# A written-out order of 1700 operations is replaced by another one, with 23 warm-up matmuls in it where there were 20

## The chip, the cores and the metric

The kernel runs on one core of one Trainium2 chip. The metric is the device time of one execution in microseconds (us), the median of three runs for the kernel before.

## The reference, cut to what matters

One transformer-like layer on a sequence of 2048 positions with 448 features, in bf16. A conditioning row `c` gives six modulation vectors; then come a windowed attention with 16 heads and a gMLP mixer, each on a modulated layernorm and added back through a gate.

```python
mod = (silu(c) @ w_mod)                 # 448 -> 6 x 448: sa, ca, ga, sb, cb, gb
h = layernorm(x) * (1 + ca) + sa
q, k, v = split(h @ wqkv)               # 16 heads of 28
p = softmax(q k^T / sqrt(28))           # only keys 0..255 positions back
x = x + ga * ((p v) @ wo)
h = layernorm(x) * (1 + cb) + sb
z = gelu(h @ w_in)                      # 448 -> 1792
z1, z2 = z[:, :896], layernorm(z[:, 896:])
g = w_sp @ z2 + b_sp[:, None]           # 2048 x 2048 over the positions
x = x + gb * ((z1 * g) @ w_out)
```

## The kernel before, in words

Everything stays on the chip between the first loads and the stores. The sequence is cut into 16 tiles of 128 positions, and these into six blocks of 1, 1, 2, 4, 4 and 4 tiles (blocks 0 to 5).

The kernel first records about 1720 operations, each with its engine, its inputs and the buffers that it takes, and then gives them out in the order of one long table, `ORDER` (lines 179 to 239). An entry `35` is operation number 35; `73.1` is operation 73 in its second form, which is mostly another engine; `71/3` also says which buffer it takes. Every engine runs its operations strictly in the order in which they stand in the table, and an operation waits by semaphore for its inputs and for the last users of its buffers. So the table decides three things: what stands behind what on each engine, which engine does a movable operation, and which buffer it uses. The DMAs stand in the queue of SyncE (SP), and two of the first ones in that of ScalarE.

The names below are those that the kernel gives its operations.

- **Start.** GpSimd (POOL) sets constants: `warm` (L539, the operand of the warm-up matmuls), `id1` (`ident`, L542), `zo0` and `zo1` (`zero_one`, L541), `one` (L540). TensorE (PE) runs `warm0` and so on, which multiply zeros and whose result nobody reads; they are recorded at lines 1257 to 1260 and depend only on the memset of `warm` and on each other. `c_cols` turns `c` into columns. `wmodA01` and `wmodA23` (L508 on SP, L510 on the queue of ACT) load the first two modulation vectors, `wqk03` and `wqkM` (L514, L515) weights, `x0`, `x0b` and `x1` (L500) the first tiles.
- **modA**, 16 operations of two matmuls of one column each, makes the first modulation vectors from the loaded weights; VectorE (DVE) turns them into `modT` (L596).
- **tr0, tr1**: normalized tiles `xn` are transposed by matmul with `ident`; ACT or DVE apply the modulation and write `hT` (L695, L700).
- **qk0, qk1, ...**: queries and keys of a block, in pieces over the feature chunks; the first read `wqk_raw` (L781), the others `WQK`, a spread-out copy that ACT, DVE and POOL make (L735 to L737). `qke` moves a result from PSUM to `QKT`. `v` and `ve` are the same for the values.
- **S, E, M, PV**: scores on PE, the exponential on ACT (L902), the mask on POOL (L905), the product with the values on PE (`arena,Vaug`). Then `oq`, `rec`, `nrm`, `oT` on DVE (L1073 to L1082; `nrm` may go to POOL), `wo` on PE and `x1_` on DVE (L1092).
- **Mixer**: second layernorm and transposes by DMA, `z2m` and `z1m` on PE, gelu on ACT (L1149, L1168), layernorm over 896 features (`l3_`, `z2n`); `woutg` (L883) multiplies the rows of `w_out_sb` by the gate `gB_sb` on POOL or DVE.
- **G**: `G<tb>_<ft>_<quarter>`, 112 operations of four matmuls of 512 columns, the product with `w_sp`, whose 32 pieces `wsp<tb>_<p>` are loaded and transposed by DMA (L1197) into `QKT`, `w_spC` and `w_spD`. Then `ga` and `gu` on DVE (L1226, L1228), the matmuls `out`, `fin` on DVE (L1248) and the stores.

PE takes its work in **four shapes**. Most matmuls use the whole array. A column-split operation is issued as four matmuls of 32 columns of weights, one beside the other (L466, L781, and all PV). A score matmul uses four strips of 28 rows. The last 64 of the 448 features give matmuls of 64 rows, `..._r`, two of which can share the array where one uses the upper and the next the lower half; they may also be done over the whole array with zeros. After the table has been read, `column_tiles` makes each whole-array operation of a free kind column-split when it stands in one stretch with PV operations:

```python
if o is not None and o.mode in (FREE, COLS):
    seg.append(o)
    continue
if any(x.mode == COLS for x in seg):
    self.cols.update(x.seq for x in seg)
```

Of the kernel before, what the change touches and what calls it, by code (L numbers as in the profile page):

```python
# [179 lines left out]
21 25 22 24 27 28 1 2 0 3 4 8 6 7 23 36 35 34 15 32 67 68 69 26 70 71/3 31 1701/0 1702 1703 1704 1705 1706 1707 1708 37/4 1709 1710 33 38 39 40/1 41  # L180
42 43 44 45 46 47 48 49 50 51 52 53 54 55 78/7 72/6 56 73.1 79 1711 1712 1713 74/1 75 58.1 62.2 63.2 125 126 127 76/0 77.1 11 182 128 129 130.1/2 60.1
65.1 61.1 5 64.1 90/3 85/4 1714 80/2 1715 95/7 96 115/1 81 86 87 116 97 117 105/0 106 98 88 91 82 92 83 93 180 99.1 183 181 84.1 184 185 66.1 89 107
108 118 57 133/7 131/6 1716 1717 94 109 119 134 500/0,0 502/1 1718 1719 1720 132.1 135/2 160/0 150/1 151 136 59 137 138 139 152 165/3 161 162 153 154
166 167 163 164 168 169 110/1 100/3 111 112 113 101 114 102 103 104 145/2 146 147 148 149 155/1 156 157 158 159 140/3 141 142 143 144 501/1,1 505/0
170/2 171 172 186 187.1/3 192/3 188.1/4 193 194 190/1 173 12 10 9 14 13 189 120/6 121 122 247 249 251 245 252 246 250 248 253 174.1 517/1,0 518/6
521/7 503 30.1 175/2 176 177 123 178 179 191.1 225/1 227 228 226 494/3 124 18 19 20 17 16 254 255 256/1 260 334 229.1 524/1,0 525/8 527/5 328 495.1
413 215/1 195/2 198 197 196 205/0 199.1 207 206 208 209.1 259.1/4 263 257.1/3 258.1/2 262 506 29 519 522 498 499 261 200/3 217 202 203 216 201 204
220/2 222 221 230/0 332 411 335 330 218.1 223.1 224 333 219.1 329 331 538/0,1 540/5 539/1 232 210/3 231 211 240/2 242 233.1 243.1 213.1 241 234.1 212
235/1 238 237 336 337 264 541/0,1 504/0 236 507 267 266 265 338 214 244 542 543 544 508/0 341/4 239.1 509 339.1/1 343 340/0 510/1 342/2 415 323/3
278/2 279 324 281 280 282 325 326 327 546/0,1 547/4 550/2 548/1 545 549 551/0 552 288/2 289 268/3 270 291 290 303/1 292 305 520/0 269 523 528 526  # L190
529/0 553/1,0 555/4 554/0 271.1 306.1 272.1 283/2 304 307 273/0 275 274 308/3 286.1 311.1 276.1 511/1 530 531.1/1 416 417 277.1 497.1 414 556/0,1 557
558 559 309 298/1 301 310 312.1 564/0 299 300 302 561 284 565 293/3 285 287 532/2 496.1 560 418 412 419 420 562 591/0,1 593/3 592/2 563 512/1 566
573/0 574 533/2 534 535 536 513 294 514 515 296 571/0 295 575.1/0 537 594/1,0 516 576/1 912 346 344 345 350.2 297.1 568 570 572 567 569 582/0 595 597
577/1 578 579 580 581 599/2,1 603/0 600/4 421 583 347.1 349.1 376/0 348.1 378 361/1 377 379.1 364.1 606/1,0 607/5 424/1 584/0 380.1 363 362 365.1
585/2 913 909 428 911 910 381/0 382 384 383 385.1 608/4 366/1 609/1,2 610 369 368 367 370.1 596 598 604/2 601/1 605 602 615/0 617 618 614 612 644/1,0
646/1 645/0 586/1 587 588 589 948 944 590 318/3 320 356/2 357 319 611 616 613 619 396/1 321.1 322 359.1 399.1 946 626/0 627 647/1,0 650 648 358 360.1
397 926/0 398 927 928 929 930 931 932 652/2,0 653/3 949 400.1 945 947 423.1/3 422.1/4 628.1/0 425.1/2 629/2 649 651 933 934 313/1 314 316 620/0 315
656/1 623 659/1,2 661/2 621 624 950 317.1 625 622 951 635/0 636 952 637/1 654/2 657/4 655 658 660/4 351/1 352 353 354 355 406/2 371/3 386/0 389.1
409.1 662/0,1 665 666 663 664 407 408 388 373 387 638/0 390.1 372 639/1 640 641 642 410.1 643 916 1433 919 1435 427 426 429 431.2 697/0,1 699/5 374
670/0 671 668 375.1 433.1 430.1 667 401/1 669 672 679/0 680 953 404.1 432 681.1/0 698/3 700/2,1 701 403 402 405.1 630/0 631 632 633 634 705/0,2 954  # L200
967 454/1 455 456 457 458.1 673/0 676 675 678 677 674 688/0 682/0 703 702 704 709/0 710/1 706/2 707/4 711 712/1,2 713/0 391/1 394 392 393 689 395.1
955.1/2 690/1 961.1/0 449/0 451 450 714/1 715/0,1 716 717 718 719 683/1 684 444/3 685 686 687 691/2 920 1434 922 956 921 464/2 466 465 467.1 452.1 453
447.1 750/0,1 752/2 446 445 726/0 434/1 727 730 731 729 708 728 968 468.1 448.1 741/0 742 957/1 751/4 753/1,2 756 435 436 437 438.1 692/0 693 694 695
696 959/2 743.1/1 744/1 973 971 969 970 757 754 755 758/0,2 759/3 722/0 723 725 762/1 459/1 462.1 724 765/1,0 460 461 463.1 972 767/0 766/5 469/2 470
721 720 732/0 974 760/0 761 763/2 764 479/3 481 480 482.1 472.1 483 768/1,0 769 733 975 734.1/1 770 439/1 471 473.1 484/0 485 486 442.1 487.1 488.1
771 772 803/2,1 804/1 735/0 917 914 962 960 958 964.1 441 440 443.1 773/0 777 774 776 775 778 785/0 786 805/3 806/0,2 809 745/1 746 747 976 965 787/0
736/0 737 738 739 740 966.1 807 808 811/2,1 815/4 788/0 748 749 977 782/0 781 779 783 784 780 794/0 816/0 984.1/1 915 918 985 812/3 813/1 810 963.1
789/1 818/1,0 820/4 819/0 790 791 792 795 793 796.1/0 474/0 476 475 477 478.1 821/0,2 822 935/1 936.1 980.1/2 830/0 827 826 829 824 856/1,0 857/5
858/2 1077/1 1078 1079 1043/2 1045 1044 1080 1046 797/1 798/3 799 1051.1 800 801 992 994 1085 995 802 996 859/0,1 860 823 814 828 489/2 1047/1 491 825
978/1 817 1060/3 861 862 863 982.2/0 925 1442 981 979 923 983 924 1444 1443 1048 1062 1049 831 490 1061 1050 1063 1068.1 838/0 839 840.1/0 1052  # L210
864/0,1 868/2 837/0 834 835 832 836 833 1098/3 1099 1064/1 1100 1066 1065 1101 492.1 990 847/0 997 993 841/1 848 869/1 865/3 866/4 867 1103.1 1067
1069 493.1 991 871/0,1 873/0 872/4 986.1 989.2 1081/0 1083 842/3 843 844 845 846 1094/1 1096 1082 1308/7 1095 998 999 1097 1084 1102.1 987 988 1086
1000 849/1 1007.1/1 1013 850/2 941.1 1001/2 1002 1008 874/2,0 1310 875 876 877 1104/1 1313/6 1315 1314 1303/3 1305 1304 1309 1338/1 1339 1340 879/0
1162/0 1158 1164 882 1311 1161 1306 1341 1342 1316 1317 1307 1165 851/2 852 853 854 855 1014 1015 1105 878 870 1003/0 883 1160 881 1159 1115/3 1116
1117 880 884 1111/2 1328/3 1329 1343/6 1113 1112 1330 1345 1163 1016 891/0 1106 892 1005/2 940 1053/0 1312 1166/2 938 893/1 1017 1055 894/0 1018 888/0
1331 1114 1346 1119.1 1118 886 1348/7 1344 1132/0 1134 885 890 887 1350 1128 1347 1120.1 1332 1004 1006 1019 1020.2/2 1009.2 1012.2 1446 1022/1 1023
# [1101 lines left out]
```

## Time and profile before

| | us |
|---|---|
| median of 3 runs | 265.5 |
| lowest and highest | 264.46, 266.9 |
| the profiled execution's own time | 266.06 |
| its span, first to last instruction | 264.3 |
| mean granted TensorE clock | 0.987 |
| PE busy | 258.9 |
| DVE busy | 162.7 |
| ACT busy | 128.9 |
| POOL busy | 102.2 |

The profile shows one execution. Its own time is 1.76 us above its span, since the time also holds what lies before the first and after the last instruction. A busy PE is not a PE at its peak: a matmul counts as busy from its start to its modelled end, and they overlap, so what a matmul costs is read from the distance between the starts of one and the next.

### The profile page before, as it was taken

How to read it: one execution, taken by the hardware profiler on the slowest of the kernel's cores; microseconds unless marked ns; L12 is line 12 of the kernel's file. 1: busy time of each engine (PE TensorE's matmuls, PEld its weight loads, DVE VectorE, ACT ScalarE, POOL GpSimd, SP SyncE). 2: the span in 40 equal slices, each digit the busy share in tenths (PEclk: the TensorE clock that was granted, in tenths of full speed). 3: DMA queues.
4: the chain of work that ended last, by engine and by line, in shares of the span. 5: the costliest groups of instructions: out<-in, count | busy, mean ns of one | idle time of the engine just before them, and what ended most of it. 6: DMA issues, size and time to landing. Idle time of an engine off the chain costs nothing.

```text
span 264.3 us, 7779 instructions
## 1 busy us (share of the span) xinstructions
PE 258.9 (98%) x3401; PEld 129.5 (49%) x3401; DVE 162.7 (62%) x392; ACT 128.9 (49%) x183; POOL 102.2 (39%) x151
## 2 busy tenths in 40 slices
PE   6999999999999999999999999999999999999996
PEld 2676554656445454544444444444444444444453
DVE  4688999879888887879796713714105344152273
ACT  4699998999999999876886100000000000000000
POOL 3469679779788968784431400000000000000000
PEclk9599999999999999999999999999999999999999
DMA  6953251972390755557999990000000000000014
GB/s 220 360 172 82 58 130 28 200 132 65 69 167 28 135 82 133 101 99 142 182 167 209 181 182 0 0 0 2 0 0 0 2 0 17 17 2 17 0 59 166
DMA packets 61022, 23.86 MB, mean 90 GB/s; under 512 B 49854, under 2 KB 60861, under 8 KB 60989
## 3 DMA queue, kind: packets, MB, share of 16 engines
q1 hardware_dynamic: 60715, 22.92, 42.0%
q8 instruction: 26, 0.43, 0.7%
q10 hardware_dynamic: 274, 0.46, 0.5%
q14 instruction: 7, 0.06, 0.1%
HBM read 9.47 MB, written 1.84 MB: 43 GB/s over the span
## 4 chain that ended last, share of the span: by engine, by line
PE 95%; DMA 2%; ACT 1%; DVE 0%; issue 0%; SPq 0%; DVEq 0%
PE ps L469 82%; PE ps L466 12%; DMA wmod_sb<-in_w_mod_dram 2%; ACT arena L902 1%; PE ps L781 1%; DVE hT L700 0%; SPq L500 0%; DVE fin L1248 0%; DVE modT L596 0%; DVEq L172 0%
## 5 line engine op out<-in xcount | busy, mean ns | idle before, releaser
L902 ACT ACTIVATE arena<-ps 128x1024 bf16<-128x1024 f32 x76 | 72.3, 1031 | 2.3 <-PE ps L469 2.1
L1226 DVE TENSOR_TENSOR tmpg<-ps,bsp_bc 128x512 bf16<-128x512 f32 x28 | 19.2, 690 | 58.4 <-PE ps L469 58.4
L469 PE MATMUL ps<-QKT,z 128*128 128x512 bf16 x224 | 51.9, 379 | 0.0
L905 POOL TENSOR_SCALAR_AFFINE_SELECT arena<-arena 128x512 f32<-128x512 f32 x60 | 40.3, 687 | 13.3 <-ACT arena L902 11.4
L469 PEld LDWEIGHTS ps<-QKT,z 128*128 128x128 bf16 x224 | 21.9, 98 | 26.2
L619 POOL TENSOR_TENSOR rs_all<-ve_all,neghalf 128x1 f32<-128x1 f32 (+2 forms) x27 | 19.3, 716 | 26.5 <-DVE ve_all L618 26.3
L469 PE MATMUL ps<-w_spD,z 128*128 128x512 bf16 x112 | 27.1, 379 | 0.0
L469 PE MATMUL ps<-w_spC,z 128*128 128x512 bf16 x112 | 26.9, 379 | 0.0
L469 PE MATMUL ps<-w_in_sb,hT 128*128 128x448 bf16 (+1 forms) x100 | 25.1, 353 | 0.0
L469 PE MATMUL ps<-hT,w_in_sb 128*128 128x512 bf16 (+1 forms) x88 | 23.6, 379 | 0.0
L469 PE MATMUL ps<-w_out_sb,z1T 128*128 128x448 bf16 (+2 forms) x119 | 23.0, 342 | 0.0
L611 DVE BATCH_NORM_STATS2 st_all<-z2raw 128x6 f32<-128x448 bf16 x32 | 18.8, 613 | 4.5 <-ACT z2raw L1149 3.2
L469 PE MATMUL ps<-hT,WQK 128*128 128x128 bf16 (+4 forms) x127 | 21.4, 299 | 0.0
L611 DVE BATCH_NORM_STATS2 st_all<-x_sb 128x6 f32<-128x448 bf16 x32 | 18.9, 614 | 0.2
L822 DVE CAST QKT<-ps 128x512 bf16<-128x512 f32 (+2 forms) x25 | 14.5, 584 | 6.1 <-PE ps L469 3.5
L1168 ACT ACTIVATE z1T<-ps 128x512 bf16<-128x512 f32 x28 | 15.6, 598 | 4.9 <-PE ps L469 4.9
L469 PE MATMUL ps<-arena,Vaug 128*32 128x128 bf16 x720 | 17.9, 221 | 0.1
L469 PE MATMUL ps<-QKT 28*64 28x64 bf16 (+3 forms) x944 | 17.7, 211 | 0.1
L469 PEld LDWEIGHTS ps<-w_spC,z 128*128 128x128 bf16 x112 | 11.0, 98 | 13.2
L1248 DVE TENSOR_TENSOR fin<-ps,x_sb 128x448 bf16<-128x448 f32 (+2 forms) x17 | 9.8, 594 | 12.2 <-PE ps L469 12.1
L469 PEld LDWEIGHTS ps<-w_spD,z 128*128 128x128 bf16 x112 | 11.0, 98 | 12.8
L469 PEld LDWEIGHTS ps<-arena,Vaug 128*32 128x32 bf16 x720 | 13.5, 95 | 6.6 <-issue 0.8
(98 smaller groups left out, 344.4 us busy)
## 6 DMA issues: line engine op xcount, KB each, us to landing
wmod_sb<-in_w_mod_dram SPq DMA_DIRECT2D x8, 224.0 KB, 4.5
w_in_sb<-in_B_w_in_dram SPq DMA_DIRECT2D x8, 224.0 KB, 3.8
out_dram<-fin SPq DMA_DIRECT2D x16, 112.0 KB, 1.7
x_sb<-in_A_x_dram SPq DMA_DIRECT2D x3, 448.0 KB, 7.8
bsp_bc<-in_B_b_sp_dram SPq DMA_DIRECT2D x1, 512.0 KB, 4.1
wqk_raw<-in_A_wqkv_dram SPq DMA_DIRECT2D x1, 452.0 KB, 6.1
wmod_sb<-in_w_mod_dram SPq DMA_DIRECT2D x1, 448.0 KB, 5.1
wmod_sb<-in_w_mod_dram ACTq DMA_DIRECT2D x1, 448.0 KB, 5.2
```

The costliest lines, as they stand in the source:

```text
L466: last = e.matmul(out_[32 * j:32 * j + 32], lhsT=lhsT[:, 32 * j:32 * j + 32], rhs=rhs, start=st, stop=sp, tile_position=(0, 32 * j), **kw)
L469: return e.matmul(out_, lhsT=lhsT, rhs=rhs, start=st, stop=sp, **kw)
L611: st = [dve("%sst%d" % (name, i), prio, dve_ns(D), lambda e, i=i, s_=s_: e.bn_stats(st_all[:, slot, t, i, :], s_()), deps, tens) for i, s_ ...
L619: r = pool(name + "rs", prio, 420 + 148 * n, lambda e: e.tensor_tensor(rs_all[:, slot, t0:t1], ve_all[:, slot, t0:t1], neghalf[:, t0:t1], ...
L781: last = e.matmul(out_[32 * j:32 * j + 32], lhsT=lhsT[j], rhs=rhs, start=st, stop=sp, tile_position=(0, 32 * j))
L822: return e.tensor_copy(QKT[:, g, cols], ps[:, ten.slot, 0:w])
L902: return P.op(name, pr, [("act", 925, lambda e: e.activation(e_out(), e_in(), ACT.Exp, scale=SCALE))], [s_op, t_exp0], tens + [pt], table= ...
L905: return pool(name, pr, pool_ns(n), lambda e: e.affine_select(out=pt32(slot_out.slot, off, dims), in_=pt32(slot_in.slot, off, dims), patte ...
L1168: g = P.op("z1g%d_%d" % (tb, ft), pr - 19, [("act", act_ns(512), lambda e: e.activation(z1T[:, ft, tb * 512:(tb + 1) * 512], ps[:, ten.slo ...
L1226: a = dve("ga%d_%d" % (tb, ft), pr, dve_ns(512), lambda e, tb=tb, ten=ten, tg=tg: e.tensor_tensor(tmpg[:, tg.slot, :], ps[:, ten.slot, :], ...
L1248: fs.append(dve("fin%s%d" % (nm, t), pr, dve_ns(c1 - c0), lambda e, t=t, ten=ten, ft_=ft_, c0=c0, c1=c1: e.tensor_tensor(fin[:, ft_.slot, ...
```

## The change

The number of warm-up matmuls goes from 20 to 23, and the first 13 of them, not the first 10, have 512 columns; the others have 256. The whole table `ORDER` is replaced. No operation's arithmetic changes. Of the table the first line is shown:

```diff
 ORDER = """
-21 25 22 24 27 28 1 2 0 3 4 8 6 7 23 36 35 34 15 32 67 68 69 26 70 71/3 31 1701/0 1702 1703 1704 1705 1706 1707 1708 37/4 1709 1710 33 38 39 40/1 41
+1 15 34 25 24 22 21 23 27 28 1701/0 1702 1703 1704 1705 1706 1707 1708 0 35 36 32 37/3 1709 1710 2 3 4 8 6 67 68 31 69 70 71/4 29 26 1711 33 38 39
...
-    for i in range(20):
-        n_ = 512 if i < 10 else 256
+    for i in range(23):
+        n_ = 512 if i < 13 else 256
```

Besides moving operations within an engine, the new table moves some to another engine: from POOL to DVE `wqkf1_3`, `hm5_0`, `h2q0_3`, `x2_4`, `x2_8`, `x2_15`, `woutg1`, `woutg2`, `woutg3`, `h2m12_1`, `h2m12_3`; from DVE to POOL `nrm0`, `nrm10`, `nrm13`, `x2_11`, `x2_14`, `woutg0`; from ACT to DVE `wqkr1_q`, `z2e1_0`, `z2e3_0`, `h2m14_2`, `h2m14_3`; from DVE to ACT `qke0_0`, `qke0_5`, `z2e0_1`, `h2m14_0`; from ACT to POOL `hm5_1`, `h2q8_0`; from POOL to ACT `h2m12_2`.

On PE, from the first warm-up on, these rows stood before (`one,crz` is `c_cols`, `sc_sb,wmod_sb` is modA, `ident,xn` are the transposes tr0, `hT,wqk_raw` and `hT,WQK` pieces of qk0):

```order
L469 MATMUL ps<-warm 128x512 x8
L469 MATMUL ps<-one,crz 128x1 x4
L469 MATMUL ps<-warm 128x512 x2
L469 MATMUL ps<-sc_sb,wmod_sb 128x1 x32
L469 MATMUL ps<-ident,xn 128x128 x2
L469 MATMUL ps<-warm 128x256 x3
L469 MATMUL ps<-ident,xn 128x128 x2
L781 MATMUL ps<-hT,wqk_raw 32x128 x8
L469 MATMUL ps<-warm 128x256
L781 MATMUL ps<-hT,wqk_raw 32x128 x4
L469 MATMUL ps<-warm 128x256
```

The same place on PE in the new order:

```order
L469 MATMUL ps<-warm 128x512 x8
L469 MATMUL ps<-one,crz 128x1 x4
L469 MATMUL ps<-warm 128x512 x3
L469 MATMUL ps<-sc_sb,wmod_sb 128x1 x32
L469 MATMUL ps<-ident,xn 128x128 x3
L469 MATMUL ps<-warm 128x512 x2
L469 MATMUL ps<-warm 128x256 x4
L781 MATMUL ps<-hT,wqk_raw 32x128 x12
L469 MATMUL ps<-ident,xn 128x128
L781 MATMUL ps<-hT,wqk_raw 32x128 x12
L469 MATMUL ps<-hT,WQK 128x128
```

Ahead of modA stands one more warm-up of 512 columns. Behind it three transposes and then six warm-ups stand together (2048 columns), where three of 256 columns stood among four transposes. Further on the new order has six warm-ups of 256 columns, the old one seven: two of each among the pieces of qk0, the others around the first scores.

At the start of POOL's queue the difference is this (a minus is the old place, a plus the new one):

```order
 L1303 MEMSET const-uint8-127 128x1
 L1284 UNCONDITIONAL_BRANCH
+L542 MEMSET ident 128x128
+L541 MEMSET zero_one 128x4
+L540 MEMSET one 128x16
 L539 MEMSET warm 128x512
-L542 MEMSET ident 128x128
-L540 MEMSET one 128x16
 L541 MEMSET zero_one 128x4
 L545 MEMSET neghalf 128x16
```

The memset for which every warm-up waits was the first of the kernel's own and is now the fourth.

The third place is on DVE late in the attention, where tiles 12 and 13 are finished. Before, these rows stood there (`oT<-o_sb` is `oT13`, `w_out_sb` a `woutg`, `x_sb<-ps,x_sb` first `x1_12` and last `x1_13`, `z_66<-ps` a `z2e`):

```order
L1092 TENSOR_TENSOR x_sb<-ps,x_sb 128x448
L618 TENSOR_SCALAR ve_all<-mv_all 128x4
L709 TENSOR_SCALAR hT<-hT,modT 128x512 x2
L1140 CAST z_66<-ps 128x448
L623 SCALAR_TENSOR_TENSOR nm_all<-mv_all,rs_all 128x4
L1078 TENSOR_TENSOR o_sb<-oq,rec_all 128x16x28
L632 TENSOR_SCALAR xn_82<-x_sb,rs_all,nm_all 128x512
L611 BN_STATS st_all<-x_sb 128x6
L1082 STREAM_TRANSPOSE oT<-o_sb 128x256
L883 TENSOR_TENSOR w_out_sb<-w_out_sb,gB_sb 128x448
L1092 TENSOR_TENSOR x_sb<-ps,x_sb 128x448
```

And now:

```order
L1092 TENSOR_TENSOR x_sb<-ps,x_sb 128x448
L1074 RECIPROCAL rec_all<-oq 128x16
L1140 CAST z_66<-ps 128x448 x2
L709 TENSOR_SCALAR hT<-hT,modT 128x512 x2
L623 SCALAR_TENSOR_TENSOR nm_all<-mv_all,rs_all 128x4
L632 TENSOR_SCALAR xn_82<-x_sb,rs_all,nm_all 128x512
L611 BN_STATS st_all<-x_sb 128x6
L883 TENSOR_TENSOR w_out_sb<-w_out_sb,gB_sb 128x448
L1082 STREAM_TRANSPOSE oT<-o_sb 128x256
L883 TENSOR_TENSOR w_out_sb<-w_out_sb,gB_sb 128x448 x2
L611 BN_STATS st_all<-z2raw 128x6
L1092 TENSOR_TENSOR x_sb<-ps,x_sb 128x448
```

Three `woutg` stand around `oT13` and ahead of `x1_13`, where there was one, and two more stand a few rows earlier; `nrm13`, the row `o_sb<-oq,rec_all`, has gone to POOL.

On SP, `wqkM` now stands ahead of `x1`, where it stood behind it, and the 32 pieces of `w_sp` come in another order. The matmuls of the two PE queues, counted by shape: 3401 before and 3476 now. Three are the new warm-ups; 24 more operations are column-split, which makes four matmuls of one; the 64-row operations go from 87 to 82; and the neighbours of unlike shape on PE go from 130 to 126.

More of the change, by code (lines that the diff above doesn't have):

```diff
@@ L184 @@
[L184 to L215, printed above, removed]
@@ new lines @@
+1586/1 1467 1468 1469 1493 1587 1494/2 1650/0 1676/7 1677 1600/5 1678 1606/6 1607 1608 1679 1479 1480 1481 1609 1527 1601 1651 1470/3 1471 1482/1
+1680/0 1528/3 1483 1681 1610/0 1495 1602 1611 1529 1546/0 1520/3 1664/2 1665 1521 1530/4 1603 1547 1604/1 1522/3 1658/1 1659 1618/0 1619 1531 1532
+1666 1620 1667 1516/6 1517 1668/2 1518/2 1669 1670/3 1588/7 1533 1589 1590 1508/5 1534/3 1535 1605 1671 1640/6 1566/2 1621 1591 1622/3 1592/2 1567
+1672 1593 1623 1568/4 1641 1673 1642 1632/7 1633 1624/4 1509 1574/2 1625 1643 1578/0 1660 1661 1575 1510/6 1511 1569 1674/3 1644/2 1645 1675 1570/3
@@ L239 @@
+1571 1662/3 1663 1576/0 1523 1519 1634/2 1682/5 1683 1636/2 1628/6 1579 1629 1637 1626/6 1684/5 1572/3 1627 1577 1573 1635 1685 1580/0 1630/1 1581
+1631 1638/5 1639 1690/4 1512/6 1513 1514/1 1691 1692/2 1686/1 1687 1688/0 1693 1515 1689 1694/6 1695 1696/5 1697/2 1698 1699 1700
 """
```

78 lines of the change are left out of this document (52 added, 26 removed).

## The prediction

> **What bounds the kernel now.** The first view is the page of the profiled execution: busy time by engine, and the chain that ended last.
>
> ```profile
> PE 258.9 (98%) x3401; PEld 129.5 (49%) x3401; DVE 162.7 (62%) x392; ACT 128.9 (49%) x183; POOL 102.2 (39%) x151
> PE 95%; DMA 2%; ACT 1%; DVE 0%; issue 0%; SPq 0%; DVEq 0%
> ```
>
> PE is busy for 98% and has 95% of the chain. Busy PE need not be dense PE, so the second view is the windows by stage (length, busy time of each engine, granted clock, DMA share, GB/s).
>
> ```profile
> 0.85:4.26 3.41, 2.90 (x7) 1.04 (x8) 1.87 (x7) 1.49 (x2) 1.53 (x8) 1.00 0.59 152
> 4.26:7.68 3.42, 2.44 (x46) 1.49 (x45) 1.13 (x6) 1.71 (x4) 0.57 (x1) 1.00 1.07 382
> 7.68:11.09 3.41, 3.20 (x47) 1.46 (x45) 2.79 (x8) 3.34 (x8) 2.49 (x4) 0.50 1.09 353
> 11.09:14.50 3.41, 3.41 (x52) 2.22 (x51) 2.38 (x11) 2.40 (x8) 0.96 (x2) 0.50 1.09 368
> 14.50:75.00 60.50, 60.35 (x1558) 34.76 (x1560) 52.80 (x127) 57.69 (x79) 47.99 (x67) 1.00 0.51 103
> 75.00:113.30 38.30, 38.19 (x986) 20.16 (x976) 31.93 (x80) 36.70 (x47) 30.40 (x41) 1.00 0.54 99
> 143.00:262.00 119.00, 118.75 (x572) 55.61 (x570) 45.69 (x93) 3.30 (x5) 3.51 (x5) 1.00 0.18 38
> ```
>
> From 14.5 us on PE has 0.15 us idle in 60.5 and 0.11 in 38.3, at the full clock. The third view, the timeline of PE, says whether that time is dense; I read the distance between starts.
>
> ```profile
> 29.41 1.91 PE L466 MATMUL ps<-hT,WQK 128*32 128x512 bf16 x32
> 31.15 0.29 PE L469 MATMUL ps<-arena,Vaug 128*32 128x128 bf16 x8
> 31.26 0.39 PE L466 MATMUL ps<-hT,WQK 128*32 128x512 bf16 x4
> 31.48 0.52 PE L469 MATMUL ps<-arena,Vaug 128*32 128x128 bf16 x24
> 31.93 0.40 PE L469 MATMUL ps<-QKT 28*128 28x192 bf16 x16
> ...
> 33.96 0.39 PE L469 MATMUL ps<-hT,WQK 64*128 64x512 bf16 x1
> 33.97 0.36 PE L469 MATMUL ps<-wv_sb,hT 64*128 64x448 bf16 x1
> 34.19 0.38 PE L469 MATMUL ps<-hT,WQK 64*128 64x512 bf16 x1
> 34.50 0.40 PE L469 MATMUL ps<-QKT 28*128 28x192 bf16 x16
> ```
>
> Eight column-split operations of 512 columns (32 matmuls) take 31.15 - 29.41 = 1.74 us, 0.217 each, and the single one at 31.26 takes 0.22: nothing waits. One PV takes 31.26 - 31.15 = 0.11. Three PV from 31.48 end at about 31.82, and the scores, another shape, start at 31.93: a **change of shape costs about 0.1 us**. The two 64-row matmuls at 33.96 and 33.97 share one slot of 0.22; the one at 34.19 has a slot of its own, 0.31 with the change of shape behind it. In the last stage 572 matmuls fill 119.0 us, 0.208 each. So behind 14.5 us the time is the number of PE slots plus the changes of shape; what remains to be won is mostly in front of it, where the clock stands at 0.50 for 6.8 us.
>
> **The start.** The chain, then PE, in order of time:
>
> ```profile
> 1.24 5.09 DMA wmod_sb<-in_w_mod_dram
> ...
> 1.36 3.31 PE L469 MATMUL ps<-warm 128*128 128x512 bf16 x8 [1.36 <-POOL warm L539]
> ...
> 6.38 0.95 PE L469 MATMUL ps<-sc_sb,wmod_sb 128*128 128x1 bf16 x32 [0.98 <-DMA wmod_sb<-in_w_mod_dram]
> 7.20 0.27 PE L469 MATMUL ps<-ident,xn 128*128 128x128 bf16 x2
> 7.31 0.49 PE L469 MATMUL ps<-warm 128*128 128x256 bf16 x3
> 7.63 0.37 PE L469 MATMUL ps<-ident,xn 128*128 128x128 bf16 x2
> 8.21 0.41 PE L781 MATMUL ps<-hT,wqk_raw 128*32 128x128 bf16 x8 [0.21 <-DVE hT L700]
> ...
> 12.46 0.63 PE L469 MATMUL ps<-ident,xn 128*128 128x128 bf16 x4
> 12.89 0.63 PE L469 MATMUL ps<-warm 128*128 128x256 bf16 x2
> 13.45 0.40 PE L469 MATMUL ps<-QKT 28*128 28x128 bf16 x8
> ...
> 14.40 0.78 PE L469 MATMUL ps<-hT,WQK 128*128 128x128 bf16 x10
> ```
>
> Until 6.34 us everything waits for the modulation's weights; then modA, transposes, qk0 from 8.21 to 12.46, the transposes of tile 1, and qk1 at 14.40, behind which PE never waits. Three warm-ups of 256 columns took 7.63 - 7.31 = 0.32 us, 0.107 each; the two at 12.89 took twice that before the scores' change of shape. So qk0 runs at half rate without a wait.
>
> The half clock began at 7.68 and ended at 14.50, two stretches of 3.41 us. In the one that ended in the drop (4.26 to 7.68) PE streamed columns for about 1.1 us by count and rate (the end of the eighth warm-up, 0.2, the two behind `c_cols`, 0.43, two transposes, 0.11, and the three warm-ups, 0.32); that is a third. In the next (to 11.09) it streamed some 14 pieces of 128 columns and two warm-ups at half rate, 1.9 us or 57%, and stayed slow. In the last (to 14.50) 2.7 us or 80%, and in the first (0.85 to 4.26) 2.90 or 85%; both were followed by the full clock. So the threshold for release lies between 57 and 80% here.
>
> [...]
>
> **The change, part by part.**
>
> *POOL's start.*
>
> ```profile
> 0.78 0.52 POOL L539 MEMSET warm<- 128x512 bf16 x1 [0.29 <-POOLq L1303]
> 1.25 0.20 POOL L542 MEMSET ident<- 128x128 bf16 x1
> 1.39 0.11 POOL L540 MEMSET one<- 128x16 bf16 x1
> 1.44 0.10 POOL L541 MEMSET zero_one<- 128x4 f32 x1
> 1.47 0.11 POOL L545 MEMSET neghalf<- 128x16 f32 x1
> ```
>
> Three memsets ahead of `warm` put it back by 1.47 - 1.25 = 0.22 us; the first warm-up starts at 1.58. Eight at half rate (3.31 us in the row) end by 4.9, `c_cols` and three at 0.217 by 5.6. All of it is hidden behind the transfer that lands at 6.34: **0**; without that cover it would be 0.22 + 0.217.
>
> *Six warm-ups between the transposes and qk0.* The three transposes end at 7.36; 2048 columns at full rate are 0.86 us, to 8.22, just when `hT` is there (8.21): nothing. If the clock falls at 7.68, 0.54 us of them are left and take 1.08, so that qk0 starts at 8.76: **+0.55**. In qk0 the new order has ten changes of shape, the old one twelve (-0.25 at half rate), and one transpose within it (+0.1). If nothing else changed, tile 1 would follow at 12.86, 0.4 later.
>
> But the warm-ups fill the stretch from 7.68: 1.08 us without a hole, then 2.33 us of qk0 with 64% streaming (its rate before, 1.83 us in 2.88), 2.57 of 3.41, 75%. That is nearer to 80, where the clock came back, than to 57. I take it that it **returns at 11.09**. Then the 1.77 us left of qk0 take about 0.95, tile 1 comes at 12.05, and of the 1.94 us from there to qk1 the matmuls' share halves (about -0.3; the eviction of `hT` stays): qk1 at some 13.7 instead of 14.40. The term is **-0.7**; bounds +0.4 and, if the clock never falls, -1.4 (rival C).
>
> *PE's slots behind it.* Counted in the new order: the 24 operations now column-split cost what they cost whole (0.217 against 0.216). Of the 64-row pieces of the projections, 27 in 16 slots become 22 in 13, and five go whole: two slots more, +0.4. Changes of shape 130 to 126: -0.4. The scores stand within 0.3 us of PE work of where they stood. Sum **0**, bounds -0.4 and +0.4.
>
> *Moved evictions, masks and norms.* DVE gains some 2.5 us in all, ACT loses 2. What hides that is DVE's idle time, 17% in the row of 75 to 113.3, and PE's other work; without the cover, rival B. ACT, busy for 57.69 of 60.5, is relieved, which can win nothing while PE is dense. **0**.
>
> *SP's queue.* `wqkM` lands earlier and `x1` later by one issue, about 0.5 us; both have slack as long as qk0 is slow. In the mixer `G3_2_0`, the first user of `w_spD`, stands 33 parts of G earlier.
>
> ```profile
> 126.75 0.34 SPq L869 DMA_DIRECT2D bsp_bc<-in_B_b_sp_dram  x1
> ...
> 152.40 4.60 SPq L1197 DMA_TRANSPOSE w_spD<-in_B_w_sp_dram  x3
> ...
> L469 PE MATMUL ps<-w_spD,z x112: 379/379/379, 184.3 to 252.3; 128*128 128x512 bf16 x112
> DMA to landing us min/median/max: 3.2/4.1/6.3
> ```
>
> It moves from 184.3 to about 184.3 - 33 x 0.863 = 155.8. Its pieces come twelve transposes behind `bsp`; 20 took 127.1 to 157.0, 1.5 each: issued by 145, landed by 151 at the slowest. Slack 4.5 us: **0**.
>
> *Sum.* 266.06 - 0.7 = 265.4 against the profiled execution. That one lies 0.56 above the median; how the stretches of the clock fall is a draw in each execution, and I take half of this off: **265.1 us**.
>
> **The rivals.**
>
> *A. The clock still comes back at 14.50,* and the warm-ups are in qk0's way at half rate. For it: the threshold may be 80%. Against: 75% is nearer to what sufficed. 266.06 + 0.4 = 266.5.
>
> *B, slower: DVE becomes the bound between 85 and 104 us.*
>
> ```profile
> 85.00:104.00 19.00, 18.98 (x475) 9.96 (x466) 16.46 (x39) 18.44 (x23) 15.48 (x22) 1.00 0.61 115
> ...
> 103.52 0.76 DVE L883 TENSOR_TENSOR w_out_sb<-w_out_sb,gB_sb 128x448 bf16<-128x448 bf16 x1
> ```
>
> Four more `woutg` there, at 0.62 to 0.76 us, add 2.7; `z2e` and `nrm13` cancel. 16.46 + 2.7 = 19.2 in a stage of 19.0. It decides from where DVE's lag (x1_13 at least 1.3 us later) exceeds the PE work that stands ahead of its users. At worst all is passed on: 266.06 + 2.7 = 268.8. Against it: the tiles that wait, 12 and 13, feed `z2m12` and `z2m13`, which PE reaches some 20 us later.
>
> *C. The warm-ups hold the clock,* and it never falls. qk0 from 8.23 takes half of 4.25, but tile 1 waits for `x1`, on which DVE's queue stands, to 11 to 11.5; qk1 at 13.0: -1.4, 264.7, and 263.1 in an execution as far below as the lowest run of before. Against it: 4.26 to 7.68 gains only one warm-up and two thirds of another, about 1.5 us of 3.41.
>
> *D. Nothing differs,* the stretches falling as they like: 265.5; it lies within the forecast.
>
> **How the numbers follow.** Forecast (with D) 0.49, A 0.22, B 0.09, C 0.20. The range goes from C, 263.0, to A with the highest run of before (0.84 above the profiled one), 267.4; it leaves out B and the corners of C. About 1%, 2.65 us, can be told from no change here. Faster by more, under 262.85, needs C in a lucky draw and a little more: 0.10. Slower by more, over 268.15, is B: 0.09. Within: 0.81.
>
> **What the changed profile would show.** Right: the first warm-up at 1.58; modA still at 6.38; a half clock that lasts one stretch of 3.41 us, or none; qk1 near 13.7; 0.863 per part of G, and idle PE under 0.5 us from there to the end. A shows two stretches and qk1 later than 14.4. B shows PE waiting for `x_sb`, `oT` or `hT` from DVE around 90 to 110 us. The prediction is wrong if the new order makes PE wait in the attention, where I have only the positions, or if the clock also falls behind 14.5.

## The result, and the profile after

| | before | after |
|---|---|---|
| median of 10 executions each, us | 266.69 | 268.6 |
| lowest and highest | 263.61, 269.19 | 266.63, 270.38 |
| the profiled execution | 266.06 | 269.32 |
| its span | 264.3 | 267.6 |
| its mean granted clock | 0.987 | 1.000 |

The ratio is 1.011, with a 95% interval from 1.0074 to 1.0146. The changed kernel is slower, by about 1%; I had forecast 265.1 us, and the median lies above my range too. (The ratios here are of means, without executions that were disturbed as a whole, so they differ a little from the ratio of the medians, here 1.007.)

The page first, busy time and chain, as they were shown of before:

```profile
PE 259.2 (97%) x3476; PEld 129.6 (48%) x3476; DVE 167.6 (63%) x398; ACT 128.1 (48%) x181; POOL 99.6 (37%) x147
PE 90%; DVE 4%; DMA 2%; issue 2%; SPq 1%; ACT 0%
```

PE is as busy as before and a smaller part of the chain, in which "issue" now has 2%: time in which PE waited for nothing that the profile shows. DVE's 4% are some 3 us at the start and 6.5 us from 94.9 to 101.4, where the chain runs over DVE; PE itself waited for DVE only 0.17 us at the end of that stretch. The windows of the changed kernel tell where (columns as before: length, PE, PEld, DVE, ACT, POOL, clock, DMA share, GB/s):

```profile
7.68:11.09 3.41, 3.41 (x79) 1.97 (x77) 3.01 (x11) 3.16 (x9) 1.68 (x3) 1.00 1.09 351
14.50:75.00 60.50, 57.73 (x1507) 33.14 (x1505) 50.42 (x120) 54.36 (x71) 45.24 (x62) 1.00 0.58 121
75.00:113.30 38.30, 37.12 (x979) 19.00 (x980) 34.84 (x78) 34.82 (x42) 30.23 (x39) 1.00 0.41 78
143.00:262.00 119.00, 119.00 (x569) 55.00 (x568) 45.50 (x93) 4.68 (x7) 4.46 (x7) 1.00 0.15 35
```

The half clock at 7.68 is gone. But PE stands idle for 2.77 us between 14.5 and 75 and for 1.18 between 75 and 113.3, where before it was 0.15 and 0.11. The last stage is as dense as it was. PE's timeline at the start of the changed kernel:

```profile
1.60 3.60 PE L469 MATMUL ps<-warm 128*128 128x512 bf16 x8 [1.60 <-POOL neghalf L545]
...
5.32 1.46 PE L469 MATMUL ps<-warm 128*128 128x512 bf16 x3
6.57 1.00 PE L469 MATMUL ps<-sc_sb,wmod_sb 128*128 128x1 bf16 x32
...
7.61 1.03 PE L469 MATMUL ps<-warm 128*128 128x512 bf16 x6
8.57 0.35 PE L781 MATMUL ps<-hT,wqk_raw 128*32 128x128 bf16 x12
...
11.44 0.40 PE L469 MATMUL ps<-ident,xn 128*128 128x128 bf16 x4
...
12.86 2.11 PE L469 MATMUL ps<-hT,WQK 128*128 128x128 bf16 x35 [0.25 <-DVE nm_all L649]
```

The three warm-ups from 5.32 to 6.57 still ran at half rate (0.42 us each, where 512 columns took 0.217 in the profile before); the six from 7.61 to 8.57, 2048 columns in 0.96 us, ran near the full one (0.87 by the 0.217). qk1 (the last row) comes at 12.86 us, 1.5 earlier than the 14.40 of the profile before. So against that profile the start brought what rival C gave it, and the attention lost some 3.7 us. The largest pieces of the chain that are called "issue" (start, length), and PE's timeline around the longest:

```profile
28.40 0.77 issue
42.16 0.50 issue
65.57 1.38 issue
86.15 0.44 issue
```

```profile
64.36 1.05 PE L466 MATMUL ps<-hT,WQK 128*32 128x512 bf16 x16
65.23 0.34 PE L469 MATMUL ps<-arena,Vaug 128*32 128x128 bf16 x9
66.95 0.76 PE L469 MATMUL ps<-arena,Vaug 128*32 128x128 bf16 x39 [1.38 <-issue]
```

PE stops in the middle of the PV of one tile and goes on after 1.38 us with the same kind of matmul; no engine is late for it. What is special about these places is their number in PE's stream of instructions. The next rows are windows from 0 to the middle of six such stalls; what counts is the number of matmuls and of weight loads, the x behind PE and PEld:

```profile
0.00:28.90 28.90, 26.55 (x473) 16.15 (x474) 21.69 (x70) 24.04 (x50) 18.29 (x35) 1.00 0.77 215
0.00:42.40 42.40, 39.54 (x856) 23.55 (x856) 33.79 (x97) 35.49 (x64) 28.72 (x49) 1.00 0.69 182
0.00:56.80 56.80, 53.68 (x1237) 31.39 (x1238) 45.31 (x123) 48.80 (x79) 39.35 (x65) 1.00 0.64 159
0.00:66.50 66.50, 62.34 (x1492) 36.04 (x1492) 53.33 (x138) 57.30 (x88) 46.81 (x74) 1.00 0.67 165
0.00:76.50 76.50, 71.82 (x1747) 41.14 (x1747) 60.94 (x155) 65.58 (x98) 53.54 (x84) 1.00 0.63 150
0.00:86.30 86.30, 81.30 (x2002) 45.80 (x2002) 68.82 (x174) 75.22 (x108) 61.69 (x95) 1.00 0.63 146
```

474, 856, 1238, 1492, 1747, 2002: the steps are 382, 382, 254, 255 and 255 weight loads, just under 3, 3, 2, 2 and 2 times 128. A matmul with its load is two instructions (3476 of each here), so the steps are multiples of 256 instructions; what is missing are the semaphore instructions in the stream. With these counted, the first instruction behind each of the six is number 962, 1729, 2498, 3009, 3521 and 4033: always 193 or 194 beyond a multiple of 256. And the DMA queue that carries instructions moves 16,384 bytes in a packet; in the 1.2 us from 64.5 it moved one, which ended at 65.64, 1.31 us ahead of PE's going on:

```profile
q8 instruction: 1, 0.02, 5.5%
```

That gave theory F (fetch): PE's instructions arrive in blocks of 256, and where PE runs through short matmuls faster than the next block arrives, it stands still at the edge. Its rivals were P (the idle belongs to those operations, by waits that the trace doesn't show) and D (the prediction's rival B, DVE late in the attention).

### The profile page after: what moved, and what is told of

The parts are those of the page before. It is cut to its first block, busy times and chain, and to the rows that moved or that the text cites. A ratio compares the mean times of both kernels' runs of the same rounds, so it can differ in the third digit from the quotient of the medians.

```text
span 267.6 us, 7927 instructions
## 1 busy us (share of the span) xinstructions
PE 259.2 (97%) x3476; PEld 129.6 (48%) x3476; DVE 167.6 (63%) x398; ACT 128.1 (48%) x181; POOL 99.6 (37%) x147
## 4 chain that ended last, share of the span: by engine, by line
PE 90%; DVE 4%; DMA 2%; issue 2%; SPq 1%; ACT 0%
PE ps L469 77%; PE ps L466 13%; DMA x_sb<-in_A_x_dram 2%; DVE st_all L611 1%; SPq L517 0%; DVE x_sb L1092 0%; DVE oq L1073 0%; ACT arena L902 0%; DVE ve_all L618 0%; DVE w_out_sb L883 0%; SPq L500 0%; DVE xn L632 0%; DVE hT L700 0%; DVE WQK L735 0%; SPq L515 0%
## 5 line engine op out<-in xcount | busy, mean ns | idle before, releaser
L469 PE MATMUL ps<-arena,Vaug 128*32 128x128 bf16 x720 | 18.9, 221 | 1.5 <-issue 1.4
L611 DVE BATCH_NORM_STATS2 st_all<-x_sb 128x6 f32<-128x448 bf16 x32 | 19.2, 615 | 0.6 <-DMA x_sb<-in_A_x_dram 0.4
L466 PE MATMUL ps<-hT,WQK 128*32 128x512 bf16 (+1 forms) x236 | 17.8, 373 | 1.0 <-issue 0.8
L469 PE MATMUL ps<-hT,WQK 128*128 128x128 bf16 (+4 forms) x117 | 18.5, 290 | 0.3 <-DVE nm_all L649 0.3
L469 PEld LDWEIGHTS ps<-arena,Vaug 128*32 128x32 bf16 x720 | 14.3, 95 | 8.7 <-issue 1.9
L469 PEld LDWEIGHTS ps<-QKT 28*128 28x128 bf16 (+1 forms) x944 | 11.5, 97 | 11.5 <-ACT arena L902 4.8
```

Source lines behind the costliest of these rows:

```text
L466: last = e.matmul(out_[32 * j:32 * j + 32], lhsT=lhsT[:, 32 * j:32 * j + 32], rhs=rhs, start=st, stop=sp, tile_position=(0, 32 * j), **kw)
L469: return e.matmul(out_, lhsT=lhsT, rhs=rhs, start=st, stop=sp, **kw)
L611: st = [dve("%sst%d" % (name, i), prio, dve_ns(D), lambda e, i=i, s_=s_: e.bn_stats(st_all[:, slot, t, i, :], s_()), deps, tens) for i, s_ ...
```

## The experiments

"Edge stalls" below are idle pieces of PE that end at an instruction 193 or 194 beyond a multiple of 256 and 1.2 to 1.6 us behind the end of a packet of the instruction queue, counted from 0.1 us on, less the 0.217 us that the starts of two matmuls of 512 columns lie apart anyway. By that measure the profile before has none of them and the profile after six, 3.7 us in all.

**1. The changed kernel, its warm-ups of 512 columns in pieces of 128.**

```diff
-  mm(e, ps[:, w_ten.slot, 0:n_], warm[:, 0:128], warm[:, 0:n_], True, True)
+  [mm(e, ps[:, w_ten.slot, k:k + m_], warm[:, 0:128], warm[:, k:k + m_], True, True)
+   for m_ in [128 if n_ == 512 else n_] for k in range(0, n_, m_)][-1]
```

> The changed kernel, with each of its 13 warm-ups of 512 columns given out as four of 128 columns: the same columns and the same order, but 39 matmuls (78 instructions of PE, with their weight loads) more ahead of modA, all while PE waits for the modulation's weights. Theory F (fetch): the idle pieces of PE that wait for nothing shown, some 4.7 us in all, come where PE runs through about 315 instructions faster than a block of 256 of them (16,384 bytes on the instruction queue) is brought in, so they depend on how many instructions stand ahead. Then they leave their places, the one of 1.55 us ahead of PV7_m0 among them, and by the same budget of 4.8 us for 315 instructions they sum to about 2.5: 266.3 us, 2.3 less than after's 268.6. Theory P (place): they belong to operations and to waits that the trace doesn't show; then they stand at the same operations with the same lengths, and the time is 268.6 within 0.5. Theory D (DVE late in the attention): also 268.6.

Measured: 269.01 us; ratio to before 1.0121 (1.008 to 1.0162). The time missed theory F's number, the places did not. PE's timeline at two of the new stalls, and windows that end in three of them:

```profile
56.51 0.51 PE L469 MATMUL ps<-arena,Vaug 128*32 128x128 bf16 x21 [1.02 <-issue]
...
64.52 0.59 PE L469 MATMUL ps<-QKT 28*64 28x64 bf16 x50
65.74 0.26 PE L469 MATMUL ps<-QKT 28*64 28x64 bf16 x14 [0.63 <-issue]
```

```profile
0.00:56.00 56.00, 51.68 (x1234) 33.66 (x1238) 43.06 (x120) 47.61 (x78) 38.35 (x63) 1.00 0.68 159
0.00:65.30 65.30, 60.27 (x1489) 38.44 (x1492) 50.40 (x136) 55.28 (x86) 45.68 (x73) 1.00 0.72 167
0.00:79.40 79.40, 73.63 (x1870) 45.89 (x1875) 62.45 (x162) 68.22 (x101) 55.81 (x88) 1.00 0.68 153
```

PE stops in the middle of one score operation, between the fiftieth and the fifty-first of its 64 equal matmuls, where no data can be awaited. The weight loads ahead are 1238 and 1492, the same numbers as in the changed kernel (PE's own column lacks some records here), though 39 matmuls stand ahead that were not there; the third, 1875, lies just under three times 128 further on, at a block edge where the changed kernel did not stop. The four other edges at which the changed kernel stopped have no such stall here. So the stalls stay at multiples of 256 and change their operations, and PV7_m0 has none. Theory P falls. The edge stalls sum to 2.2 us, near the 2.5 expected; another 1.38 us came at 25.5 us, where PE waited for DVE's `hT` (L709), which itself started 2.7 us behind anything shown (1.1 in the changed kernel). The semaphores of the trace say what DVE waited for: the last of the four DMA transposes that fill this `hT` landed at 26.57 us, 4.2 us after its issue (2.9 in the changed kernel), and `hT` started at 26.66. So this piece is a late transfer and no stall of instructions; why it was late stays open.

**2. The kernel before, its warm-ups in pieces of 128** (the same edit).

> The kernel before, with each of its 10 warm-ups of 512 columns given out as four of 128: 30 matmuls (60 instructions) more ahead of modA. Theory F: idle pieces without a shown cause appear in the attention where there was one of 0.21 us; by the budget of 4.8 us for 315 instructions they sum to about 4.4, 3 more than it gives for before itself: 269.7 us against 266.7, with 2.0 to 4.0 for the difference. Theories P and D: no new idle piece, 266.7 within 0.5.

Measured: 267.35 us; 1.0066 (1.0034 to 1.0098). Stalls appeared at instructions 1729, 2242, 2498, 3522 and 4802, 2.1 us in all, for 60 instructions that run in a wait. The sign is F's, the size half of what I gave. Since the operations and their order are those of before, the profiled execution can be held against that of before weight load by weight load: it loses 2.7 us between the start of the attention and the end, in steps that lie in the main at these five places.

**3. The changed kernel without `column_tiles`.**

```diff
     P.schedule()
-    P.column_tiles()
     P.emit(handles, dma_sems)
```

> The changed kernel without column_tiles: the 277 operations that it makes column-split stay whole, so PE has 2954 matmuls instead of 3476 and 192 changes of shape instead of 124. At 0.1 us each these add 6.8 us. Theory F: PE runs through its instructions more slowly everywhere, and no idle piece over 0.2 us without a shown cause is left: -4.7, in sum 270.7 us. Theory P: the pieces stay, 275.4. Theory D: PE is later everywhere, so DVE's part (at most 1 us) goes and the rest stays, about 274.5.

Measured: 270.96 us, 1.0214 (1.0173 to 1.0255), a quarter of a microsecond from F's sum. No edge stall is left, and the longest wait of a PE matmul for nothing shown falls from 1.4 us to 0.3. The rows (us in all, times, longest), first of the changed kernel, then of this one:

```profile
PE ps L469 <- issue: 2.3, 3, 1.4
PE ps L466 <- issue: 0.8, 1, 0.8
```

```profile
PE ps L469 <- issue: 1.3, 7, 0.3
```

**4. The new start, the old order behind it.** The table is the first 145 entries of the new one, then what is left of the old one in its own order.

> The changed kernel's start, its first 145 entries up to the first scores of tile 0, and behind it everything in the order of before. Instructions ahead of the attention: 6 more than before. If the start is worth 1.4 us and the loss lies wholly behind it (theories F, P and D agree): 265.3 us, with idle pieces without a shown cause under 0.5 us in all. If the start is worth nothing and the loss is smaller than I think: 266.7.

Measured: 264.85 us, 0.9989 (0.9955 to 1.0024); edge stalls 0.4 us. The loss lies behind the start. What the start is worth is taken up in experiment 14.

**5 and 6. G in short matmuls, to measure the fetch by itself.** In before, with w = 128 and then w = 64:

```diff
-  last = mm(e, ps[:, ten.slot, :], z2[...], w_spT(si, tb), si == 0, si == NT - 1)
+  m_ = w if 0 < si < NT - 1 else 512
+  for k in range(0, 512, m_):
+      last = mm(e, ps[:, ten.slot, k:k + m_], z2[...], w_spT(si, tb)[:, k:k + m_], si == 0, si == NT - 1)
```

> The kernel before, with the matmuls of G given out in pieces of 128 columns of w_sp instead of 512 (the first and last of each sum stay whole): 98 of 112 becomes four, the same columns in the same order, 2,408 more weight loads and as many more matmuls. Theory F now says: in the 24 fetches of 16,384 bytes that a trace shows, from the moment when PE stands at instruction 256k+135 to the end of the fetch and 1.3 us more it takes 3.5 to 6 us, and PE needs the block at instruction 256(k+1)+193, 314 instructions later. Pieces of 128 columns (0.054 us for two instructions) make that 8.5 us: no stall in G, and the time of before within 0.6 us. Theory P: the same. It is the control of the next run.

> The same with pieces of 64 columns: 5,488 more matmuls than before, the same columns. 314 instructions then take about 4.2 us where all are small and 4.7 with the whole ones between. Theory F: PE stalls at many of the 25 block edges in G, always where the number of its instructions is 193 or 194 beyond a multiple of 256, by 0.2 to 0.4 us in the mean: 5 us longer than before, 2 to 9. Theory P (the idle pieces belong to operations of the attention and to waits not shown): no stall in G, the time of before within 0.6 us, or the same excess at each small matmul, if a weight load takes longer than 64 columns.

Measured, one execution each: 268.44 and 273.38 us against 265.26. Both numbers are off. The extra time is in the main no stall, but spread over the matmuls: 3.2 us / 2408 = 1.3 ns and 8.1 / 5488 = 1.5 ns for each one more. The traces give it without the start, which ran at half rate in the second (qk1 at 13.92 us, 12.01 in the first): from the same weight load, at 141 to 143 us, to the last one before takes 118.7 us, these two 121.7 and 126.3, and the second without its stall 125.6 (the trace of experiment 13), so 1.2 and 1.3 ns. Only one edge stall came in G, at instruction 6593, again 193 beyond a multiple of 256, while the last pieces of `w_sp` still arrived:

```profile
156.83 1.10 PE L469 MATMUL ps<-QKT,z 128*128 128x64 bf16 x32
158.39 0.79 PE L469 MATMUL ps<-QKT,z 128*128 128x64 bf16 x21 [0.46 <-issue]
```

So 314 instructions in 5.0 us (627 ran in the 10 us from 175 to 185) did not stop PE at the other edges; nor did 314 in 3.7 us in the profile before, 81.51 to 85.21 us. The 4.2 us of the expectation was an estimate. What differs is the fetch: reckoned from PE's instruction 256k+135 (a point that I fitted), it starts after a median of 1.2 us here behind 200 us, and of 2.2 in the attention, where it ranged from 0.9 to 6.0 in the 286 fetches of the 16 traces.

**7. `woutg1`, `woutg2`, `woutg3` on POOL again** (three entries of the new table: `938.1`, `939.1`, `940.1` become `938`, `939`, `940`).

> The changed kernel, with woutg1, woutg2 and woutg3 done by POOL again, at the same places of the table; nothing else. PE's instructions stay as they are. Theory D (DVE, three gate multiplications fuller between 85 and 104 us, holds PE up): the waits of PE at 87.7 and 101.1 us go, and the time falls by 1 us or more, to 267.6 or less. Theory F: at most 0.4 us of 268.6, and the stalls stay at the same block edges.

Measured: 269.0 us, 1.0135 (1.0073 to 1.0197): nothing gained. PE's waits at 87.7 and 101.1 us stayed, at 0.15 and 0.21 us (0.26 and 0.17 in the changed kernel). The run by itself tests theory D only in part: of the three multiplications one ran in that stage (0.79 us at 101.34), the two others from 108.3 on. What rules D out is that PE waited for DVE 0.2 us there, in either kernel. The longest stall stood where it was, to 0.03 us:

```profile
66.92 0.76 PE L469 MATMUL ps<-arena,Vaug 128*32 128x128 bf16 x39 [1.38 <-issue]
```

**8. The old start, the new order behind it** (the converse of 4, cut after 130 entries).

> The converse of the mixed order tried before: the start of before (its first 130 entries, to the first scores of tile 0) and behind it everything in the order of the changed kernel. Instructions ahead of the attention: 6 fewer than in the changed kernel. If the new order behind the start carries the whole loss: as slow as the changed kernel or slower by what its start is worth (0.3 to 1.4 us): 268.9 to 270.0. If the loss came only of how the two parts of the new order lie together: near before, 266 to 267.

Measured: 267.98 us, 1.0076 (1.0036 to 1.0115). The new order is slow behind the old start too, though 0.9 us less than I gave at least; its edge stalls, 3.3 us, stand at 962, 1729, 2498, 3009 and 3521, the same instructions as in the changed kernel and in 7.

**9. Fewer column-split operations in the changed kernel.** In `column_tiles`:

```diff
-                self.cols.update(x.seq for x in seg)
+                at = [k for k, x in enumerate(seg) if x.mode == COLS]
+                lo = at[0] if at[0] >= 4 else 0
+                hi = at[-1] + 1 if len(seg) - 1 - at[-1] >= 4 else len(seg)
+                self.cols.update(x.seq for x in seg[lo:hi])
```

> The changed kernel, but column_tiles leaves whole those operations that stand four or more in a row at an end of a stretch: 190 operations column-split instead of 277, 3215 matmuls instead of 3476, 138 changes of shape instead of 124. The added changes cost 14 x 0.1 = 1.4 us. Theory F: PE needs a block of 256 instructions less often in just these stretches; about half of the 3.7 us of fetch stalls goes (1 to 3): 268.1 us, between 267.0 and 269.1, with the stalls left at 193 or 194 beyond a multiple of 256. Without the fetch it would be 268.6 + 1.4 = 270.0.

Measured: 267.89 us, 1.0075 (1.0045 to 1.0106), with edge stalls of 2.1 us at 2242 and 2753. The time is near what I expected: 261 matmuls fewer come with 1.6 us less of stalls, against 14 changes of shape more. That the version is faster than the changed kernel is not shown, since the two intervals overlap.

**10, 11 and 12. Only the place of the edges moved**, by warm-ups in pieces of 64 columns: in before, in the changed kernel, and in the mixed order of 4.

```diff
-  lambda e, n_=n_: mm(e, ps[:, w_ten.slot, 0:n_], ...)
+  lambda e, n_=n_, m_=(64 if n_ == 512 else n_): [mm(e, ps[:, w_ten.slot, k:k + m_], ...)
+                                                  for k in range(0, n_, m_)][-1]
```

(in the mixed order `64 if i < 17`.)

> The kernel before with each warm-up of 512 columns as eight of 64: 70 matmuls, 140 instructions more ahead of modA. If 314 instructions are held against the fetch times that the traces show, drawn at random, the stalls of the attention sum to 2 us more than in before as it is (1 to 3): 267.6 us against 265.6. If before were merely free of dense stretches, nothing would change.

> The changed kernel with each of its 13 warm-ups of 512 columns as eight of 64: 182 instructions more ahead of modA. By the same calculation 0.8 us less than the changed kernel, and no place of the block edges is free of stalls for it: 267.8 us, between 266.8 and 268.8. If only an unlucky place of the edges made the changed kernel slow, this or the version with pieces of 128 columns would come down to 265.

> The new start with the old order behind it (measured at 264.85 us), with its first 17 warm-ups in pieces of 64 columns, 206 instructions more ahead of modA, which moves the block edges by 50 instructions. By the calculation with the traces' fetch times 0.4 us less: 264.4 us, between 263.8 and 265.4; the version from which I expect the lowest time.

Measured: before with 140 instructions more 268.02 us, 1.0101 (1.0057 to 1.0144); the changed kernel with 182 more 267.93, 1.0087 (1.0053 to 1.012); the mixed order with 206 more 266.89, 1.0056 (1.0025 to 1.0087), where I expected a gain. In the profiled executions of the last two the edge stalls sum to 1.9 us (one single stall, at instruction 3265) and 1.3. The first is the plainest run of the study: the old order, each operation at its place, and 1% lost like the changed kernel. PE's timeline at its three edge stalls:

```profile
54.60 0.36 PE L469 MATMUL ps<-arena,Vaug 128*32 128x128 bf16 x11
55.83 0.36 PE L469 MATMUL ps<-arena,Vaug 128*32 128x128 bf16 x12 [0.87 <-issue]
...
74.35 0.67 PE L469 MATMUL ps<-QKT 28*64 28x64 bf16 x60
75.67 0.22 PE L469 MATMUL ps<-QKT 28*64 28x64 bf16 x4 [0.65 <-issue]
...
96.73 0.87 PE L469 MATMUL ps<-arena,Vaug 128*32 128x128 bf16 x47
98.33 0.22 PE L469 MATMUL ps<-arena,Vaug 128*32 128x128 bf16 x1 [0.73 <-issue]
```

They stand at 2498, 3522 and 4802 and sum to 2.2 us. Held against the profile of before weight load by weight load, this execution loses 4.0 us between the start of the attention and the end: steps of 1.1, 0.9 and 1.0 us at these three edges (some of it won back right behind), 1.4 at 25 us, and behind 100 us nothing, to 0.02 us. The 1.4 is again a late DMA transpose ahead of DVE's `hT`: it landed 4.5 us after its issue, 3.1 in the profile before. So the old order lost at all three places of its edges that I tried besides its own (60, 140 and, with the new start, 206 instructions further on) and not with 6 more instructions ahead (4 and 14); the new one was slow at all three places tried (268.6, 269.0, 267.9).

**13. Traffic beside G in pieces of 64 columns.** 32 loads that nobody reads, three under way at a time, given out behind the mixer:

```diff
+    for i in range(32):
+        h, q = i % 2, (i // 2) % 4
+        junk.append(load("junk%d" % i, 999, lambda e, h=h, q=q: e.dma_start(w_in_sb[:, 2 * h:2 * h + 2, q * D:(q + 1) * D],
+            B_w_in[192 * h:192 * h + 256, q * D:(q + 1) * D].rearrange("(c p) n -> p c n", p=128)), 256 * D * 2,
+            mixed + junk[-3:][:1] * (i > 2)))
```

> The version with G in pieces of 64 columns, and 32 loads of 224 KB in G that nobody reads (the weights w_in_sb once more, three under way at a time), some 30 to 40 us of transfers. Theory F with traffic: while they run, the fetch starts 2 us and more after its trigger instead of 1.2, so that fetch and 1.3 us behind it come near the 4.2 us that 314 instructions take: stalls of 0.2 to 1 us at several of the 8 to 10 block edges there, 1 to 4 us in sum, 274.5 to 277.5 us against 273.4. If the traffic has no part in it: no stalls, 273.4.

Measured, one execution: 271.01 us, 2.4 less than without the loads and outside both forecasts. Held against experiment 6 weight load by weight load, 1.8 us of this are the start, which ran at half rate there and at the full one here, and 0.6 the stall at 6593, which is missing here; everywhere else the two agree to 0.04 us. The windows, first without the loads, then with them (the last two columns are DMA share and GB/s):

```profile
175.00:185.00 10.00, 9.79 (x313) 9.41 (x314) 1.81 (x3) 0.00 (x0) 0.00 (x0) 1.00 0.02 5
```

```profile
175.00:185.00 10.00, 10.00 (x317) 9.41 (x314) 2.92 (x5) 0.00 (x0) 0.00 (x0) 1.00 0.69 191
```

The eight fetches from 160 to 195 us started after a median of 1.8 us instead of 1.3, but none came too late: the closest edge was passed 1.49 us behind its packet's end. So beside these loads the fetch started 0.5 us later; that traffic alone makes the stalls of the attention is not shown.

**14. The mixed order of 4 once more.**

> The new start with the old order behind it once more, for a narrower interval: 264.8 us, ratio to before 0.995 to 0.999, since in the executions of before whose clock stays at 1.0 (most of them) the new start can save only about 0.3 us, and 1.4 in the others.

Measured: 264.7 us against 264.98, ratio 1.0001 (0.9971 to 1.003): the new start gains nothing that can be measured. PE's timeline says why, first before's start in an execution without the half clock (the trace of experiment 5, equal to before up to G), then the new start:

```profile
5.78 0.95 PE L469 MATMUL ps<-sc_sb,wmod_sb 128*128 128x1 bf16 x32
7.61 0.30 PE L781 MATMUL ps<-hT,wqk_raw 128*32 128x128 bf16 x8 [0.30 <-DVE hT L700]
10.79 0.38 PE L469 MATMUL ps<-ident,xn 128*128 128x128 bf16 x4 [0.23 <-DVE mv_all L614]
12.01 2.39 PE L469 MATMUL ps<-hT,WQK 128*128 128x128 bf16 x36
```

```profile
5.95 0.95 PE L469 MATMUL ps<-sc_sb,wmod_sb 128*128 128x1 bf16 x32
7.89 0.35 PE L781 MATMUL ps<-hT,wqk_raw 128*32 128x128 bf16 x12
11.32 0.40 PE L469 MATMUL ps<-ident,xn 128*128 128x128 bf16 x4 [0.51 <-POOL xn L632]
12.64 2.18 PE L469 MATMUL ps<-hT,WQK 128*128 128x128 bf16 x36 [0.16 <-DVE hT L700]
```

Without the half clock the old start reaches qk1 at 12.01 and the new one at 12.64: the six warm-ups stand in the way for 0.1 us, and DVE's queue stands on `x1`, which now lands behind `wqkM`, to 9.68 us (0.21 us idle), before it turns to tile 1's norm (L649 at 10.23, 9.62 in the old start). The mean granted clock of each timed execution says how often a fall is recorded: below 0.998 in 20 of 82 executions of before (median 266.3 us; 264.9 for the others), and in 4 of 54 of the kernels with the new start as it stands. The mean doesn't catch every slow start: it reads 1.000 in the execution of experiment 6, equal to before up to G, where PE ran its start at half rate and qk1 came at 13.92, 1.9 us later than in experiment 5. So how often the start of before is slow I can't say; at least 20 times in 82.

No version that I ran beats both kernels; 4 and 14 equal before.

## Why the prediction was wrong

- **The step that failed is "PE's slots behind it", sum 0.** It counted column-split operations by their columns ("cost what they cost whole") and asked nothing of the number of instructions. The term that was missing is the fetch of PE's instructions: 3.7 us in the profile after, none before, and up to 1.9 us at a single edge (experiment 11). 72 of the 75 matmuls that came with the change are those 24 column-split operations. What tells against blaming these alone is experiment 10: the old order loses 1% too when its edges move, 2.2 us of it in edge stalls and 1.4 in a late transfer. In these runs the term changed with three things: how many instructions stand in a stretch (no edge stall in 3, 2.1 us in 9, 3.7 in the profile after), where the multiples of 256 fall (2.1, 2.2 and 1.3 us in 2, 10 and 12; none in before, 0.4 in 4), and how late the fetch starts (a median of 1.2 us in 6 behind 200 us, 2.2 in the attention; in 13, beside the loads, 1.8 against 1.3, but with no stall). The shares of the first two in the 2 to 3 us of the change I can't separate.
- **The six warm-ups, -0.7:** the trace did what rival C said: no fall of the clock, tile 1 at 11.44 (I had 11 to 11.5), qk1 1.5 us earlier than in the profile before. Whether the clock would have come back after one stretch or two, which I estimated from 57 and 80% in the one profile before, was so not put to the test, and no other run shows such a threshold. But I took a fall of the clock for a property of the kernel where it was the draw of one execution. In 62 of 82 executions of before the mean clock shows none (and misses some), and over all of them the new start gains nothing that can be measured (14). "I take half of this off" was 0.28 of what should have been all of the 0.7; no run shows this 0.28, and that the fall is a draw I took without one; what the runs showed is a fall in 20 of 82.
- **POOL's start, 0:** right in the trace of 14, where modA's first matmul starts together with its weight load, at 5.95. The first warm-up started at 1.60, 1.58 was said. In the profile after it was not wholly hidden: the weights were there at 6.21, and the first matmul started at 6.57, behind the third warm-up. I had given the three behind `c_cols` 0.217 us each, and there they took 0.42.
- **SP's queue, 0:** `w_spD` cost nothing, as said. That `x1` has slack "as long as qk0 is slow" was right, and qk0 was not slow: then tile 1 comes half a microsecond later (10.79 against 11.32 in 14).
- **Moved evictions, 0, and rival B:** B's 268.8 is near the result by luck. DVE was busy for 17.32 us of the 19 from 85 to 104, not 19.2: of its five `woutg` in the changed kernel three ran behind that stage, from 107.4 us on. PE waited for DVE 0.2 us there, and with three `woutg` back on POOL the time was the same (7).
- **What would show it wrong** named PE waiting in the attention "where I have only the positions". That is where it was; but the positions were enough to count 256 by 256, and I did not.
- Of the 5.1 us between the profiled executions of the changed kernel (269.32) and of 14 (264.26), edge stalls explain 3.6 and the start 0.2; the remaining 1.2 us I did not take apart.

## What to carry to other kernels

Where PE has no data to wait for, count its instructions too, not only its columns: here five of the six edge stalls of the profile after came behind 314 instructions that ran in 3.7 to 4.5 us without the stall (the sixth behind 6.4), and splitting a matmul in four to save a change of shape (0.1 us) costs six instructions. In these profiles such stalls were named "issue", several fell in the middle of an operation, and they appeared or moved when 60 or 78 instructions were added far ahead (2 and 1); try that before looking for a dependency, and before believing that a new order is worse, or better, by 1%. And ask whether the profiled execution is a usual one: here a mean clock below 0.998, like its 0.987, was a draw that 20 of 82 executions had.

## What the hardware showed that I had not expected

- In 286 fetches between 20 and 110 us in 16 traces, PE never passed an edge sooner than 1.21 us behind the end of its packet. Between 15 and 262 us these traces hold 27 idle pieces of PE of 0.4 us or more; two are the waits at 25 us (1 and 10), and all the 25 others ended at such an edge, 1.28 to 1.55 us behind a packet's end.
- PE stood at the edge 193 or 194 instructions beyond a multiple of 256, by the count of the trace, in each of the 12 kernels whose trace has such a stall.
- A whole matmul given out as four or eight over its columns cost 1.2 to 1.3 ns for each piece more, stalls aside (5, 6 and 13).
